# One DRAIN on GpSimd in front of the last expert's output DMAs, in an attention and mixture-of-experts kernel

## The chip, the core and the metric

The kernel runs on one core of one Trainium2 chip. The metric is the device time of one execution in microseconds (us). Each core has five engines with an instruction queue each: TensorE (PE: matrix products, with PEld for its weight loads), VectorE (DVE), ScalarE (ACT), GpSimd (POOL) and SyncE (SP, which here only issues DMAs). Engines wait for each other and for DMAs through semaphores. In a profile a name with a "q" behind it (POOLq, SPq) means an instruction that the engine's sequencer handles by itself, such as a DRAIN or a wait for semaphores; these are not counted as busy time.

## What is computed

An attention without softmax, normalised by its root mean square, and behind it a layer of eight experts. Each token goes to one expert, by sorted scores, and no expert takes more than N/E = 576 tokens:

```python
kv = np.einsum('bhsd,bhse->bhde', k, v)            # batch 8, heads 8, seq 576, head_dim 64
out = np.einsum('bhsd,bhde->bhse', q, kv)
x = out / np.sqrt(np.mean(out * out, axis=-1, keepdims=True) + 1e-06) * g_norm
...
logits = x @ w_gate                                # N, D, E, F = 4608, 512, 8, 1024
order = np.argsort(-logits.flatten())              # greedy: best score first, 576 per expert
...
for e in range(E):
    mask = assigned == e
    h = np.maximum(x[mask] @ w1[e], 0.0)
    out[mask] = h @ w2[e]
```

All data are float32.

## The kernel before

The attention runs first and leaves its result in DRAM as `x_dram`. Then the experts run one after the other, `t` = 0 to 7, while the search for the next expert's tokens runs beside them. `layers(t)` is one expert: 576 tokens in five blocks of rows (four of 128 and one of 64), a first product with `w1` (in `one_layer`, line 1243), ReLU on ScalarE (line 1218), and a second product with `w2` (`second`, line 1203). Both products are done in quarters after Winograd's form of Strassen's scheme: seven products of halves take the place of eight, for which sums and differences of the quarters have to be made first.

Those sums are GpSimd's work: of `w1` (`weight_sums`, tile `sw`, line 1088), of `w2` (`sum_w2`, tile `tw`, line 1166) and of the hidden layer (`sums`, tile `sh`, line 1195). GpSimd also issues all indirect DMAs: five gathers of token rows for each expert (line 990, `xg<-x_dram`) and five scatters of finished rows for each expert (`put`, line 1171, `out_dram<-y_sb` or `y_rest`). That is 40 + 40 = 80 DMAs in the program. SyncE issues the plain DMAs, mostly of weights.

For TensorE, VectorE, ScalarE and SyncE the order of work is the order in which the program is written. For GpSimd it is written by hand: `in_order` links each of its instructions behind the one before, without a semaphore. Nothing else decides its order.

The change lies in `layers`, between the first and the second half of an expert. Behind `one_layer` the last two sums of `tw` are issued (`sum_w2(t, len(tw_of[t][1]))`), and then the second products run, in the order `m` = 1, 2, 6, 5, 64, 7, 4, 3 for the last expert. Product 64 is the block of 64 rows (line 1311); its result `y_rest` goes out by the first `put`. Products 4 and 3 finish the other four blocks, with a `put` each. For the last expert there are no gathers of a next one, so that behind the last two `tw` sums GpSimd's queue holds only these five `put`s and the end of the program.

The end of the program is not written in the kernel. The tool chain puts it there (line 1428 in the profile): each engine executes a DRAIN, SyncE first waits for the semaphores of all DMAs, and then all engines meet in a barrier; GpSimd clears the semaphores, and they meet once more.

Of the kernel before, what the change touches and what calls it, by code (L numbers as in the profile page):

```python
# [26 lines left out]
def kernel(  # L27
# [11 lines left out]
    nc = tc.nc  # L39
# [4 lines left out]
    E, _, F = moe_w1.shape  # L44
# [841 lines left out]
    def in_order(made):  # L886

        if on_pool:
            tc.add_manual_dep(made.ins, on_pool[-1],
                              mybir.DependencyInfo(mybir.DependencyClass.NoSync, mybir.DependencyReason.SCHED_ONLY),  # L890
                              reason="order on GpSimd")
        on_pool[:] = [made.ins.name]
# [285 lines left out]
    def layers(t):  # L1178
# [113 lines left out]
        for i in range(FH):  # L1292
            summed.pop((t, i))
        weights.pop(t)

        y_of = [moe.tile([P, 2, DM], FT, name="y_sb", tag="y", bufs=2) for _ in range(2)]

# [57 lines left out]
    with tc.manual_schedule(engines={PE, DVE, ACTE, SPE}):  # L1355
# [31 lines left out]
        for t in range(E):  # L1387
            after = None
            for used in layers(t):
                if used == 0:  # L1390
                    next(turning)
                    continue
                if used is None:

                    if t + 1 < E:
                        while listed <= t:
                            search()
                        after = after or (turn if t + 1 < RELAID else turn_relaid)(t + 1)
                        wait += next(after) or 0.0
                    continue  # L1400
                wait -= used
                while wait <= 0 and search():
                    pass
            done, turning = t, after
# [28 lines left out]
```

## Time and profile before

| | us |
|---|---|
| median of 3 runs | 632.99 |
| lowest, highest | 629.66, 642.17 |
| the profiled execution | 632.92 |
| its span, from the first to the last instruction | 631.1 |
| PE busy in the span | 591.7 (94%) |
| DVE, ACT, POOL busy | 395.0, 200.3, 386.6 |
| indirect DMAs on POOL | 80, of 0.91 to 1.35 us for the outgoing ones |
| mean granted TensorE clock | 0.966 of full speed |

The span is what the trace shows; the 1.8 us between it and the execution's own time lie around it. Busy time counts work of the engines alone. A tail in which only sequencers have instructions shows no busy engine, so it has to be read from the rows of the line that ends the program, with start and duration of each DRAIN. A DMA has two times: that of the instruction that issues it on GpSimd, and its landing, which is given apart, from the issue on.

### The profile page before, as it was taken

To read this page: it belongs to the slowest core of one execution; us is meant where nothing else is said; L and a number is where in the kernel's file an instruction comes from. 1 tells how busy PE (TensorE), PEld (TensorE's weight loads), DVE (VectorE), ACT (ScalarE), POOL (GpSimd) and SP (SyncE) were. 2 spreads that over 40 slices of the span, in tenths; PEclk is the share of its full clock that TensorE was granted. 3 is DMA by queue.
4 is the path that set the end of the run, shared out by engine and by line. 5 is a ranking of instruction groups with operands and counts; after the bars stand their busy time and mean duration, and the time that the engine had idled before them with its cause. 6 is when DMAs were issued, how large, how long until landed. Compare 5 with 4: busy or idle time off the path is not lost.

```text
span 631.1 us, 12717 instructions
## 1 busy us (share of the span) xinstructions
PE 591.7 (94%) x4844; PEld 459.0 (73%) x4844; DVE 395.0 (63%) x1262; ACT 200.3 (32%) x428; POOL 386.6 (61%) x402
## 2 busy tenths in 40 slices
PE   8998999349999999999999999999999999999993
PEld 4777887226787678777867787778678877877873
DVE  4466669776786778579648867876993452242211
ACT  1565667913321222223222322231223213222310
POOL 0136444005875598479747886876778688788532
PEclk9999999559999999999999999999999999999998
DMA  8999999438018208224521574458145662731001
GB/s 274 296 323 308 318 315 357 175 119 269 6 37 310 71 2 270 79 69 133 164 81 44 171 205 148 136 190 209 42 168 183 176 204 69 219 110 43 2 8 66
DMA packets 60733, 100.46 MB, mean 159 GB/s; under 512 B 4608, under 2 KB 30208, under 8 KB 60160
## 3 DMA queue, kind: packets, MB, share of 16 engines
q1 hardware_dynamic: 54080, 80.75, 39.3%
q0 software_dynamic: 5888, 18.88, 9.3%
q8 instruction: 38, 0.62, 0.4%
q14 instruction: 23, 0.19, 0.1%
q10 hardware_dynamic: 704, 0.02, 0.1%
HBM read 76.04 MB, written 23.59 MB: 158 GB/s over the span
## 4 chain that ended last, share of the span: by engine, by line
PE 82%; DVE 8%; issue 4%; DMA 2%; POOL 2%; ACT 1%; POOLq 0%; SPq 0%; DVEq 0%; ACTq 0%
PE x_ps L1243 14%; PE x_ps L1203 12%; PE z_ps L1243 10%; PE y_ps L1243 9%; PE y_ps L1203 8%; PE z_ps L1203 7%; PE o_ps L494 4%; PE y_ps L1311 4%; PE qt_ps L382 3%; PE kv_ps L397 3%; DMA v_sb<-in_v_dram 2%; PE t_ps L1102 1%; PE given_ps L679 1%; PE warm_ps L916 1%; PE given_ps L674 1%
## 5 line engine op out<-in xcount | busy, mean ns | idle before, releaser
L1248 ACT COPY h<-x_ps 128x288 f32<-128x288 f32 x93 | 37.1, 399 | 169.0 <-PE x_ps L1243 163.6
L1243 PE MATMUL x_ps<-xs,sw 128*128 128x288 f32 x248 | 71.2, 409 | 0.4 <-DVE xs L1115 0.4
L1088 POOL TENSOR_TENSOR sw<-w_sb 128x256 f32<-128x256 f32 x64 | 46.8, 731 | 35.5 <-DMA w_sb<-in_moe_w_dram 21.1
L1203 PE MATMUL x_ps<-tw,sh 128*128 128x256 f32 x256 | 60.7, 383 | 0.0
L1243 PEld LDWEIGHTS x_ps<-xs,sw 128*128 128x128 f32 x248 | 46.3, 190 | 13.7 <-issue 1.1
L1171 POOL DMA_INDIRECT out_dram<-y_sb,outs x32 | 32.3, 1010 | 33.7 <-DVE y_sb L1347 25.2
L1203 PEld LDWEIGHTS x_ps<-tw,sh 128*128 128x128 f32 x256 | 47.4, 190 | 7.0 <-issue 0.8
L1195 POOL TENSOR_TENSOR sh<-hid 128x512 f32<-128x512 f32 x32 | 40.6, 1270 | 18.5 <-ACT hid L1218 18.5
L1218 ACT ACTIVATE hid<-hid 128x576 f32<-128x576 f32 x64 | 43.8, 686 | 23.3 <-DVE hid L1257 13.8
L530 POOL TENSOR_TENSOR xo<-o_sb,inv 128x512 f32<-128x512 f32 x27 | 28.4, 1079 | 33.1 <-DVE inv L517 33.1
L990 POOL DMA_INDIRECT xg<-x_dram,ids x40 | 38.1, 952 | 15.5 <-issue 9.9
L1166 POOL TENSOR_TENSOR tw<-w_sb 128x512 f32<-128x512 f32 x32 | 40.0, 1274 | 6.7 <-DMA w_sb<-in_moe_w_dram 6.6
L1341 ACT COPY u<-x_ps 128x512 f32<-128x512 f32 x24 | 14.0, 585 | 91.8 <-PE x_ps L1203 71.1
L494 PE MATMUL o_ps<-kvx,qt 64*128 64x72 f32 (+1 forms) x640 | 39.2, 271 | 1.9 <-issue 1.9
L494 PEld LDWEIGHTS o_ps<-kvx,qt 64*128 64x128 f32 (+1 forms) x640 | 34.5, 178 | 7.4 <-issue 6.5
L1243 PE MATMUL z_ps<-xt,sw 128*128 128x288 f32 x128 | 38.3, 415 | 0.1
L1243 PE MATMUL x_ps<-xt,w_sb 128*128 128x288 f32 x124 | 37.6, 416 | 0.5 <-ACT xt L1107 0.5
L1243 PE MATMUL y_ps<-xt,w_sb 128*128 128x288 f32 x128 | 37.0, 409 | 0.0
L1243 PE MATMUL z_ps<-xs,sw 128*128 128x288 f32 x128 | 36.8, 409 | 0.0
L1243 PE MATMUL y_ps<-xs,w_sb 128*128 128x288 f32 x128 | 36.5, 407 | 0.0
L507 DVE TENSOR_REDUCE ms<-sq 128x8 f32<-128x512 f32 x36 | 24.3, 682 | 18.6 <-ACT sq L500 18.2
L1203 PE MATMUL z_ps<-w_sb,sh 128*128 128x256 f32 x128 | 31.9, 390 | 0.5 <-DVE y_sb L1337 0.5
(315 smaller groups left out, 1313.2 us busy)
## 6 DMA issues: line engine op xcount, KB each, us to landing
w_sb<-in_moe_w_dram SPq DMA_DIRECT2D x32, 512.0 KB, 6.8
w_sb<-in_moe_w_dram SPq DMA_DIRECT2D x8, 2048.0 KB, 8.5
k_sb<-in_k_dram SPq DMA_DIRECT2D x16, 576.0 KB, 5.8
v_sb<-in_v_dram SPq DMA_DIRECT2D x16, 576.0 KB, 5.7
q_sb<-in_q_dram SPq DMA_DIRECT2D x16, 576.0 KB, 5.6
x_dram<-xo SPq DMA_DIRECT2D x16, 512.0 KB, 3.9
bounce<-xg SPq DMA_DIRECT2D x4, 1024.0 KB, 4.0
xr<-bounce SPq DMA_DIRECT2D x16, 256.0 KB, 4.7
```

Source lines behind the costliest of these rows:

```text
L494: nc.tensor.matmul(o_ps[rows_at, rp, (2 * r2 + l) * W:(2 * r2 + l + 1) * W], lhsT=turned_q[bn][ks, l, block // 2:block // 2 + m].rearrange ...
L530: nc.gpsimd.tensor_tensor(xo[:, t], o_sb[:, t, :, 0:D], inv[:, t * H:(t + 1) * H].rearrange("p (h o) -> p h o", o=1).to_broadcast([P, H, D ...
L990: tokens = nc.gpsimd.indirect_dma_start(out=xg[0:nr, n], out_offset=None, in_=x_dram, in_offset=bass.IndirectOffsetOnAxis(ap=ids[0:nr, n:n ...
L1088: in_order(nc.gpsimd.tensor_tensor(o, x, y, op=op))
L1166: in_order(nc.gpsimd.tensor_tensor(o, x, y, op=AL.subtract))
L1171: put = nc.gpsimd.indirect_dma_start(out=out, out_offset=bass.IndirectOffsetOnAxis(ap=ids_of[t][0:nr, n:n + 1], axis=0), in_=y_sb[0:nr, :] ...
L1195: in_order(nc.gpsimd.tensor_tensor(o[:, ms], x[:, ms], y[:, ms], op=op))
L1203: nc.tensor.matmul(p_ps[:, n], lhsT=left[:, f, n * P:(n + 1) * P], rhs=right[:, f], start=first, stop=(f == FH - 1), skip_group_check=True)
L1218: nc.scalar.activation(both, both, ACT.Relu)
L1243: nc.tensor.matmul(p_ps, lhsT=lhs[:, r], rhs=rhs[:, r], start=(m in (1, 2, 4, 5) and r == 0), stop=(r == 1), skip_group_check=(m in (6, 7, ...
L1248: nc.scalar.copy(u, p_ps)
L1311: nc.tensor.matmul(y_ps[l * nr:(l + 1) * nr], lhsT=hid[:, l * FH + f, a:a + nr], rhs=w2[:, l * FH + f, :], start=(f == 0), stop=(f == FH - 1))
```

## The change

For the last expert alone (`t + 1 == E`), one `drain` is issued on GpSimd. It is put in GpSimd's written order with `in_order`, behind the last two `tw` sums and in front of the five output DMAs. It has no semaphore to wait for, and no other instruction waits for it. The instructions of all engines, their order and their waits are otherwise the same as before.

```diff
@@ -1292,6 +1292,8 @@
         for i in range(FH):
             summed.pop((t, i))
         weights.pop(t)
+        if t + 1 == E:
+            in_order(nc.gpsimd.drain())
 
         y_of = [moe.tile([P, 2, DM], FT, name="y_sb", tag="y", bufs=2) for _ in range(2)]
```

## The prediction

> **What bounds the kernel now.** I read the page's chain by engine first, to see what sets the 631.1 us as a whole, and then only the last 40 us, because that is where the change sits.
>
> ```profile
> PE 82%; DVE 8%; issue 4%; DMA 2%; POOL 2%; ACT 1%; POOLq 0%; SPq 0%; DVEq 0%; ACTq 0%
> ```
>
> TensorE carries the span. The change adds and moves nothing on TensorE, so it can be worth something only in the few us in which TensorE is not working. Next, busy time by stretches, from the last hidden sums to the end (columns: length, then busy us of PE, PEld, DVE, ACT, POOL with counts, clock, DMA share, GB/s):
>
> ```profile
> 592.00:604.00 12.00, 12.00 (x57) 10.45 (x56) 1.92 (x4) 2.69 (x5) 7.43 (x6) 1.00 0.01 2
> 604.00:612.00 8.00, 8.00 (x37) 4.68 (x36) 0.67 (x1) 0.84 (x2) 0.00 (x0) 1.00 0.00 0
> 612.00:624.00 12.00, 9.49 (x43) 7.71 (x41) 2.24 (x5) 0.59 (x1) 4.76 (x5) 1.00 0.22 76
> 624.00:631.10 7.10, 0.00 (x0) 0.00 (x0) 0.00 (x0) 0.00 (x0) 0.00 (x0) 0.58 0.10 37
> ```
>
> Two things are to be seen. In the last 7.1 us no engine computes at all. And between 604 and 612 GpSimd does nothing, while TensorE is busy for every one of the 8 us. The timeline of GpSimd gives the order there (start, us, what, idle before):
>
> ```profile
> 601.31 2.49 POOL L1166 TENSOR_TENSOR tw<-tw,w_sb 128x512 f32<-128x512 f32 x2
> 612.29 0.91 POOL L1171 DMA_INDIRECT out_dram<-y_rest,outs  x1 [8.50 <-DVE y_rest L1319]
> 618.77 0.98 POOL L1171 DMA_INDIRECT out_dram<-y_sb,outs  x1 [5.57 <-DVE y_sb L1347]
> 620.06 0.96 POOL L1171 DMA_INDIRECT out_dram<-y_sb,outs  x1 [0.31 <-issue]
> 621.33 0.96 POOL L1171 DMA_INDIRECT out_dram<-y_sb,outs  x1 [0.30 <-issue]
> 622.75 0.95 POOL L1171 DMA_INDIRECT out_dram<-y_sb,outs  x1 [0.47 <-DVE y_sb L1337]
> ```
>
> The last sum ends at 601.31 + 2.49 = 603.80. The first output DMA cannot go before 612.01, when `y_rest` is written (VectorE, 611.33 + 0.68). The last output DMA is issued by 623.70. The tile view of the output in this window gives its landing:
>
> ```profile
> DMA to landing us min/median/max: 2.6/2.7/2.7
> ```
>
> So the data is in memory at 622.75 + 2.7 = 625.45, and yet the span runs to 631.1. What fills it are instructions of the sequencers, which do not count as busy. The view of line 1428 (end of the program; duration min/median/max in ns, first and last start):
>
> ```profile
> L1428 SPq EVENT_SEMAPHORE  x12: 17/28/28, 624.0 to 631.1; - x12
> L1428 POOLq EVENT_SEMAPHORE  x4: 17/17/17, 630.4 to 631.0; - x4
> L1428 POOLq DRAIN  x3: 40/107/7797, 622.5 to 630.9; - x3
> ```
>
> **GpSimd's closing DRAIN lasts 7797 ns**, from 622.5 to 630.3. The same view cut to 624 to 630 shows what else happens:
>
> ```profile
> L1428 SPq EVENT_SEMAPHORE  x10: 17/28/28, 624.0 to 626.0; - x10
> L1428 SPq DRAIN  x2: 7/7/7, 626.0 to 626.1; - x2
> ```
>
> SyncE has checked every DMA by 626.1 and then stands still until 630.4. The list of waits gives SyncE a wait of 4.4 us "for PEq", but TensorE was long done; GpSimd's DRAIN is what came last. So 630.3 − 626.1 = 4.2 us of the end belong to this DRAIN alone.
>
> **What the Trainium skill says.** "PSUM — Partial Sum Buffer", Engine vs sequencer instructions: a drain waits for the engine to go fully idle. The trace agrees that it waits, and shows more: the DRAIN goes on for 630.3 − 623.7 = 6.6 us after GpSimd's last recorded work. "Perfetto Trace Analysis", Sequencer-only Instruction: the time reported for a DRAIN is its execution, waits on semaphores not included; so the 7797 ns are work or waiting inside the DRAIN. "VectorE: DVE Perf Modes", The DRAIN you can't avoid, gives the closing DRAINs on all engines as about 12 ns. The trace has 7 to 19 ns for the later ones on the other engines, but 40 and 107 ns on GpSimd behind the long one, and 7797 ns for that one; the measurement decides. "DMA: Bandwidth & Descriptors", Anatomy of one DMA: about 2.0 us plus the bytes at 436 GB/s, an estimate of 2.6 us for the 256 KB of one output DMA; the trace has 2.7.
>
> **The change, part by part.** One instruction is added on GpSimd, behind the last two `tw` sums and in front of the five output DMAs of the last expert. No instruction of another engine moves, nothing waits for the DRAIN on another engine, and the DRAIN waits for no semaphore. Behind it on its queue stand only the five output DMAs and the closing DRAIN.
>
> (a) What the long DRAIN pays for. The first DRAIN of the program, before any DMA was issued, lasted little:
>
> ```profile
> L1419 POOLq DRAIN  x1: 188/188/188, 0.3 to 0.3; - x1
> ```
>
> So a DRAIN has no large fixed price (188, 107, 40 ns). Landing explains it up to 625.45; 630.3 − 625.45 = 4.85 us are left, in which no engine and no output transfer has anything to do. I choose: it is bookkeeping that has piled up over the kernel and is done by the next DRAIN, whichever that is. The likely unit is the indirect DMA: 40 gathers, 32 + 8 output DMAs, 80 in all. Counted from the landing that is 4.85 / 80 = 0.061 us each; counted from GpSimd's last work, 6.6 / 80 = 0.083 us each. It is not paid behind each DMA: issues stand 1.27 us apart, and a sum follows an output DMA within 1 us (561.78, then 562.77).
>
> (b) What the early DRAIN costs. 75 of the 80 DMAs stand in front of it: 75 x 0.061 = 4.6 us, or 75 x 0.083 = 6.2 us. It can end only when the sums have, at 603.80, so it ends at 608.4 to 610.0. Bounds: from nothing (it finds nothing to do) to the full 7.8 us, which gives 611.6. All lie ahead of 612.01, so it costs 0. The cover is GpSimd's idle time under TensorE's `x_ps`, `z_ps` and `y_ps` products. If that cover were overrun, the first output DMA would slip, and it has another 618.54 − 613.21 = 5.3 us before it is in the second's way.
>
> (c) What the closing DRAIN becomes. Five DMAs: 5 x 0.061 = 0.3 us behind the landing, so 625.45 + 0.3 = 625.8. That is ahead of SyncE's 626.1, which now is last. The part behind it (two barriers and the clearing of semaphores), 631.1 − 630.3 = 0.8 us, stays. Span: 626.1 + 0.8 = 626.9.
>
> Sum: 631.1 − 626.9 = **4.2 us** less. A gain above this is excluded, since SyncE's checks don't depend on the DRAIN. Against the profiled execution's own time, 632.92 (1.8 us around the span): 632.92 − 4.2 = 628.7. That execution is 0.07 us below the median of the three runs, 632.99, so the forecast against the median is the same, **628.7**. It is 0.7%; about 2% is what a measurement of this kernel can tell from no change.
>
> **Rivals.** (1) *The tail belongs to the last DMAs.* The 4.85 us are a fixed price of closing behind an output DMA just issued, or the early DRAIN returns at once and clears nothing. For it: the one long DRAIN is also the only one behind fresh DMAs, so the trace of before doesn't separate the two. Against it: the landing is over, and nothing of the kind shows between DMAs. Time: unchanged, 632.9.
>
> (2) *Part of it.* Some of the 4.85 us is piled up and some is not. Half each leaves the closing DRAIN ending at 625.45 + 2.4 = 627.9 instead of 630.3: 630.5.
>
> (3) *Slower: the early DRAIN overruns its cover.* It holds GpSimd's queue, and the output DMAs behind it then bunch at 1.27 us each. The last one is late when the first goes later than 622.75 − 4 x 1.27 = 617.7, so when the DRAIN lasts over some 13.6 us from 603.80. At twice the long DRAIN, 15.6 us, it ends at 619.4; the first DMA starts 0.3 later and the last at 624.8, 2.0 us late. With the closing DRAIN as long as before: 634.9. Against it: 13.6 us is nearly twice the longest DRAIN seen, with fewer DMAs in front.
>
> **How the numbers follow.** Piled-up work, all moved: 0.72, 628.7. Part: 0.08, 630.5. Nothing: 0.14, 632.9. Slower: 0.06, 634.9. The three runs of before reach from 629.66 to 642.17, more than the effect itself. So the low end is the lowest run less the gain, 629.66 − 4.2, rounded to 625.4. The high end takes in the case of no change with 1.6 us of spread, 634.5; a lone run like the 642.17 is left out. No case reaches 2% (620.3 or 645.6) by itself; only spread could: faster 0.01, same 0.97, slower 0.02.
>
> **What would show it.** A second long DRAIN on GpSimd at the changed line, some 4.5 us or more from 603.80 and done before 612; the first output DMA still at 612.3 and the last at 622.8; the closing DRAIN about 3 us instead of 7.8; SyncE's last check at 626.1, with its barrier directly behind. I am wrong if the closing DRAIN still takes 7 to 8 us (rival 1), if the output DMAs start later (rival 3), or if the closing DRAIN shrinks and the span doesn't, which would mean that something the trace doesn't show ends there too.

## The result, and the profile after

| | before | with the DRAIN |
|---|---|---|
| median of 21 runs, us | 634.24 | 630.97 |
| lowest, highest | 629.51, 648.46 | 626.15, 636.14 |
| ratio, 95% interval | | 0.9945 (0.9921 to 0.9970) |
| span of the profiled execution | 631.1 | 629.4 |
| tail: end of VectorE's last instruction to end of span | 8.65 | 4.42 |

The ratio is worth 3.5 us of 634.24 (1.9 to 5.0 by the interval). The ratio leaves out the slow executions, those more than 1.5% above the fastest of their kernel, so it is not quite the quotient of the two medians. Both ends of the interval are gains, though single runs scatter by more than that. The last row of the table is a sharper measure, and it is used for all runs below: VectorE's last instruction ends at 622.47 before and at 625.01 with the change, and what follows is only the last output DMA and the closing of the program. The two instructions, first before, then with the change (start, us):

```profile
622.05 0.42 DVE L1337 TENSOR_TENSOR y_sb<-z_ps,u 128x256 f32<-128x256 f32 x1 [2.09 <-PE z_ps L1203]
624.58 0.42 DVE L1339 TENSOR_TENSOR y_sb<-z_ps,u 128x256 f32<-128x256 f32 x1 [2.09 <-PE z_ps L1203]
```

The added DRAIN is the only row of its line in the changed kernel (engine, count, duration min/median/max in ns, first and last start):

```profile
L1296 POOLq DRAIN  x1: 11082/11082/11082, 601.5 to 601.5; - x1
```

It has to be read beside GpSimd's timeline (start, us, what, idle before):

```profile
603.85 2.50 POOL L1166 TENSOR_TENSOR tw<-tw,w_sb 128x512 f32<-128x512 f32 x2
614.83 0.92 POOL L1171 DMA_INDIRECT out_dram<-y_rest,outs  x1 [8.48 <-DVE y_rest L1321]
625.28 0.96 POOL L1171 DMA_INDIRECT out_dram<-y_sb,outs  x1 [0.47 <-DVE y_sb L1339]
```

The sequencer reaches the DRAIN at 601.48, while the sums in front of it are still running. The last of them ends at 606.35. So of the 11.08 us the first 4.87 are a wait for the engine, and the DRAIN's own part is 612.56 − 606.35 = **6.22 us**. The first output DMA is due at 614.6, and it still shows VectorE's `y_rest` as what it waited for: the DRAIN was done 2.0 us earlier.

The end of the program in the changed kernel:

```profile
L1430 SPq EVENT_SEMAPHORE  x12: 17/28/28, 626.6 to 629.4; - x12
L1430 POOLq EVENT_SEMAPHORE  x4: 17/17/17, 628.7 to 629.3; - x4
L1430 POOLq DRAIN  x3: 46/107/3196, 625.1 to 629.2; - x3
L1430 SPq DRAIN  x3: 7/7/7, 628.6 to 628.9; - x3
```

The closing DRAIN lasts 3196 ns instead of 7797. It ends at 628.25, and SyncE's own closing DRAIN comes at 628.6: now SyncE is last. The list of SyncE's waits has, for the wait that the prediction put down to GpSimd's DRAIN, 0.5 us at most, where it had 4.4:

```profile
SPq L1430 <- DMA out_dram<-y_sb,outs: 74.7, 2, 73.2
SPq L1430 <- PEq L1430: 0.7, 2, 0.5
```

The tail is 4.23 us shorter, and yet the span only 1.7. The other 2.5 us were lost long before the change could act. Over the first 100 us, in which the attention loads its data, the windows of the two profiles (length, then busy us and count of PE, PEld, DVE, ACT, POOL, clock, DMA share, GB/s) are, first before, then with the change:

```profile
0.00:100.00 100.00, 92.97 (x2004) 74.97 (x2005) 61.34 (x199) 54.86 (x107) 37.44 (x49) 0.98 0.91 309
```

```profile
0.00:100.00 100.00, 89.91 (x1969) 74.40 (x1978) 61.43 (x196) 52.80 (x103) 36.25 (x48) 0.97 0.91 303
```

TensorE has 35 matmuls fewer on record by then (10 of them are missing from the whole profile). Compared instruction by instruction, VectorE is 2.6 us late at 103 us and 2.5 us late at the end. The change cannot have caused this, since its DRAIN starts at 601.48. It is scatter of the loading stage, which moves from run to run: in the second profile of the same kernel (experiment 7) VectorE is 0.2 us late at that place.

### The profile page after: what moved, and what is told of

Its sections match the earlier page's. It is cut to its first block, busy times and chain, and to the rows that moved or that the text cites. A ratio compares the mean times of both kernels' runs of the same rounds, so it can differ in the third digit from the quotient of the medians.

```text
span 629.4 us, 12708 instructions
## 1 busy us (share of the span) xinstructions
PE 590.6 (94%) x4834; PEld 460.2 (73%) x4844; DVE 396.2 (63%) x1262; ACT 200.6 (32%) x428; POOL 387.4 (62%) x402
## 4 chain that ended last, share of the span: by engine, by line
PE 83%; DVE 6%; DMA 4%; issue 4%; POOL 2%; ACT 1%; POOLq 0%; SPq 0%; ACTq 0%; DVEq 0%
PE x_ps L1243 15%; PE x_ps L1203 12%; PE z_ps L1243 10%; PE y_ps L1243 10%; PE y_ps L1203 8%; PE z_ps L1203 7%; PE o_ps L494 5%; PE y_ps L1313 4%; DMA v_sb<-in_v_dram 3%; PE qt_ps L382 3%; PE kv_ps L397 3%; PE t_ps L1102 1%; PE given_ps L679 1%; PE given_ps L674 1%; PE warm_ps L916 1%
## 5 line engine op out<-in xcount | busy, mean ns | idle before, releaser
L494 PE MATMUL o_ps<-kvx,qt 64*128 64x72 f32 (+1 forms) x640 | 40.5, 276 | 0.9 <-PE kv_ps L397 0.4
L494 PEld LDWEIGHTS o_ps<-kvx,qt 64*128 64x128 f32 (+1 forms) x640 | 35.9, 183 | 6.0 <-issue 4.7
```

Of the source, the lines that this page charges most:

```text
L494: nc.tensor.matmul(o_ps[rows_at, rp, (2 * r2 + l) * W:(2 * r2 + l + 1) * W], lhsT=turned_q[bn][ks, l, block // 2:block // 2 + m].rearrange ...
```

## The experiments

The theory: a DRAIN on GpSimd works off something that piles up with each indirect DMA, some 0.083 us for each, and it can be done under TensorE's products. Against it stand a fixed price of a late DRAIN, work that piles up with every GpSimd instruction or with bytes, and a tail that belongs to the last output DMAs. "From idle" below is the time from the end of GpSimd's last instruction in front of the DRAIN to the DRAIN's end, from the trace's times.

**1. A DRAIN in every expert.** The condition is dropped:

```diff
-        if t + 1 == E:
-            in_order(nc.gpsimd.drain())
+        in_order(nc.gpsimd.drain())
```

> The DRAIN stands at the same place in all eight experts. Tail means here: from the end of VectorE's last instruction to the end of the span (8.65 us before, 4.43 with the change). Piled-up work per indirect DMA (0.083 us each, counted from the moment GpSimd's last earlier instruction ends): 10 DMAs lie between two DRAINs, so 0.8 us each for the first seven (more where the last gather has not landed yet), 0.4 us for the eighth with 5 DMAs in front, the closing DRAIN as in the changed kernel, tail 4.4 us, and a time like that of the changed kernel (ratio to before 0.992 to 1.000). Piled-up work per GpSimd instruction of any kind (0.0165 us each for 402): about 1.6 us for the first DRAIN (some 100 instructions in front), 0.7 us for the eighth (43 in front). A fixed price of a DRAIN that comes late after another (6 us each, however much is in front): 6 us for each of the eight, and the time goes up by 10 us or more, since the sums behind the first seven are needed soon.

Measured: ratio 0.9945 (0.9917 to 0.9973), tail 4.42 us. The DMAs in front of each of the eight turned out to be 5, 10, 15, 10, 10, 10, 10 and 5. From idle: 0.50, 0.90, 3.18, 0.89, 0.89, 0.89, 0.89 and 0.48 us. The third stands right behind a gather, whose issue ends at 318.37 and which lands at 320.89; it ends at 321.54, behind that landing. In front of the others every DMA has landed before GpSimd is idle. The row of the fifth, and the sums in front of it:

```profile
L1295 POOLq DRAIN  x1: 5752/5752/5752, 432.6 to 432.6; - x1
```

```profile
434.95 2.50 POOL L1166 TENSOR_TENSOR tw<-tw,w_sb 128x512 f32<-128x512 f32 x2
```

The reader sees how little a DRAIN's duration alone says: 5.75 us, of which all but 438.33 − 437.45 = 0.89 us is waiting for sums. The fixed price falls: it would have been 6 us eight times. So does the price by GpSimd instruction: the first DRAIN has 89 instructions and 5 DMAs in front of it and takes 0.50 us (0.0165 x 89 would be 1.5), the eighth 39 and 5 and takes 0.48 (0.64 by instructions).

**2. The DRAIN in the fourth expert only.**

```diff
-        if t + 1 == E:
+        if t == 3:
```

> One DRAIN as in the change, but in the fourth expert instead of the last. Piled-up work per indirect DMA: 40 DMAs in front of it, so it lasts 40 x 0.083 = 3.3 us from GpSimd's last earlier instruction, and the closing DRAIN has the other 40 to do: it ends 3.3 us after the last output DMA was issued (6.6 before, 2.0 with the change), tail 8.65 - 3.3 = 5.3 us. If the first long DRAIN of a program pays a fixed price that later ones don't, wherever it stands: it lasts some 6 us, and the tail is that of the changed kernel, 4.4 us. If the tail belonged to the last output DMAs: tail 8.65 us.

Measured: ratio 0.9966 (0.9937 to 0.9994), tail 5.48 us. The DRAIN takes 3.36 us from idle for its 40 DMAs, and the closing one 3.43 us for the other 40. The rows of the two:

```profile
L1296 POOLq DRAIN  x1: 8228/8228/8228, 374.4 to 374.4; - x1
```

```profile
L1430 POOLq DRAIN  x3: 46/107/4618, 627.3 to 632.5; - x3
```

An early DRAIN therefore doesn't make later ones cheap as such. It does its share, and what comes after it is left to the closing one. The reading that the tail belongs to the last output DMAs falls here, since these were the same five.

**3. The DRAIN where nothing covers it**, in front of the last output DMA, and not at the place of the change:

```diff
                 if m == 3 and t + 1 == E and f == FH - 1:
                     nc.vector.tensor_tensor(quarter(0, 1)[:, n], p_ps[:, n], u_of[6][:, n], op=AL.add)
+                    if n == 1:
+                        in_order(nc.gpsimd.drain())
                     put(t, n, P, y_of[0][:, n])
```

> The DRAIN stands between the fourth and the fifth of the last five output DMAs, where nothing covers it. Piled-up work per indirect DMA: 79 x 0.083 = 6.5 us from the end of the fourth output DMA; the fifth is issued some 6.3 us later than before, lands 2.7 us behind its start, and the closing DRAIN is short: tail 10.7 us instead of 8.65, that is 2 us slower than before and 6 us slower than the change (ratio to before about 1.003). If the early DRAIN clears nothing: tail 8.7 us or a little more, as before.

Measured: ratio 1.0012 (0.9978 to 1.0046), tail 11.27 us. The time does not tell it from before; the tail does, by 2.6 us. GpSimd's timeline there:

```profile
625.48 0.96 POOL L1171 DMA_INDIRECT out_dram<-y_sb,outs  x1 [0.31 <-issue]
633.76 0.96 POOL L1171 DMA_INDIRECT out_dram<-y_sb,outs  x1 [7.32 <-issue]
```

Of the 7.32 us between the two, the DRAIN with 79 DMAs takes 6.53, as the theory had it. The rest is new: the DMA behind it begins 0.79 us after the DRAIN's end, where 0.25 had been put in, and that is why the tail is 0.5 us longer than expected. The closing DRAIN has one DMA left, which lands at 636.47. It ends at 636.56, 1.84 us from idle:

```profile
L1430 POOLq DRAIN  x3: 46/107/3012, 633.5 to 637.6; - x3
```

**4. More DMAs with hardly more rows**, and no DRAIN added. The 16 extra gathers fetch rows that nothing uses:

```diff
                 rows_of[t, n] = xg[:, n]
+                if n < 2:
+                    in_order(nc.gpsimd.indirect_dma_start(
+                        out=more[:, n], out_offset=None, in_=x_dram,
+                        in_offset=bass.IndirectOffsetOnAxis(ap=ids[0:16, n:n + 1], axis=0)))
```

> The kernel before with no DRAIN added, but with 16 more gathers of 16 rows each (two for each expert, into a tile that nothing reads): 96 indirect DMAs instead of 80, rows up by 3% only. Piled-up work per indirect DMA: the closing DRAIN ends 96 x 0.083 = 7.9 us after the last output DMA was issued (6.6 before), tail 10.0 us. Piled-up work per row or per byte: 6.8 us and 8.85. A fixed price: 6.6 us and 8.65, as before.

Measured in one run: 661.85 us, tail 9.97 us. The closing DRAIN and the last output DMA:

```profile
L1433 POOLq DRAIN  x3: 46/107/9103, 650.1 to 659.8; - x3
```

```profile
650.36 0.96 POOL L1176 DMA_INDIRECT out_dram<-y_sb,outs  x1 [0.46 <-DVE y_sb L1342]
```

From idle, at 651.32, it takes 7.91 us, to two digits what 96 DMAs were to cost. A gather of 16 rows counts as much as one of 128, so neither rows nor bytes set the price. The whole run was 24 us above the median of the runs of before beside it, 637.6, and 1.3 us of that are in the tail. Against the profile of before, VectorE's last instruction is 27.6 us late. Of this, 9.2 us are there before the first gather is issued, in the first 100 us, where this run shows a granted clock of 0.88 and before shows 0.98. The other 18 us come while the experts run, and their cause is open. Only the tail of this run is used here.

**5. The DRAIN one output DMA later**, behind the first of the last five, and not at the place of the change:

```diff
                 put(t, NB - 1, nr, y_sb)
+                if t + 1 == E:
+                    in_order(nc.gpsimd.drain())
                 continue
```

> The DRAIN stands one output DMA later than in the change: behind the first of the last five, where only the 5.3 us until the second cover it. The runs so far give a DRAIN's length from GpSimd's last earlier instruction as 0.07 + 0.0817 us for each indirect DMA since the DRAIN before. With 76 DMAs: 6.3 us, so it overruns its cover by 1.0 us; in the run with the DRAIN in front of the last output DMA the next DMA also began 0.8 us behind the DRAIN's end, instead of 0.25. So the second output DMA begins 7.1 us behind the end of the first (5.6 before), 1.5 us late; the others follow at 1.27 us each and the last begins 1.35 us later, measured from VectorE's last instruction. Tail 4.42 + 1.35 = 5.8 us; ratio to before about 0.9955. If an overrun were taken up by the 5.3 us of slack between the output DMAs (the prediction's reading): tail 4.4 us. If the DRAIN must also wait until the first output DMA has landed before it counts: 2.7 + 6.3 = 9.0 us behind the start of that DMA, tail 7.6 us.

Measured: ratio 0.9970 (0.9943 to 0.9997), tail 5.78 us. The timeline:

```profile
611.03 0.92 POOL L1171 DMA_INDIRECT out_dram<-y_rest,outs  x1 [8.47 <-DVE y_rest L1319]
619.02 0.98 POOL L1171 DMA_INDIRECT out_dram<-y_sb,outs  x1 [7.08 <-DVE y_sb L1339]
620.30 0.96 POOL L1171 DMA_INDIRECT out_dram<-y_sb,outs  x1 [0.30 <-issue]
621.57 0.96 POOL L1171 DMA_INDIRECT out_dram<-y_sb,outs  x1 [0.30 <-DVE y_sb L1339]
622.84 0.96 POOL L1171 DMA_INDIRECT out_dram<-y_sb,outs  x1 [0.30 <-issue]
```

The DRAIN ends at 618.23, 6.28 us from idle. Behind it the output DMAs run back to back at 1.27 us each, and the last is issued late. The closing DRAIN has four DMAs left. The last lands at 625.56 and the DRAIN ends at 625.77:

```profile
L1430 POOLq DRAIN  x3: 46/107/4509, 621.3 to 626.7; - x3
```

The 7.08 us of idle are put down to line 1339 on VectorE, but this DMA sends what line 1349 wrote, and that had ended at 617.24: the wait was for the DRAIN, which is not a row of this view. One DMA's place costs 5.78 − 4.42 = 1.36 us.

**6 and 8. What is last with the change.** Thirteen waits are put on SyncE's queue early, for DMAs that have long landed, so that they need not be checked at the end; the DRAIN stays (`settled` collects the last DMAs of SyncE and the output DMAs of the expert before):

```diff
                 put(t, NB - 1, nr, y_sb)
+                if t + 1 == E:
+                    for made in settled[-13:]:
+                        seen = nc.sync.nop(nofuse=True)
+                        tc.add_manual_dep(seen.ins, made.ins.name,
+                                          mybir.DependencyInfo(mybir.DependencyClass.Sync, mybir.DependencyReason.DATA),
+                                          reason="SyncE sees what has landed")
                 continue
```

> The change, and beside it 13 waits on SyncE's queue, in the program behind the last weights, for DMAs that have landed long before the end. The closing list of checks then is four instead of nine behind the last output DMA. If SyncE's checks are what ends last in the changed kernel, the end now follows the closing DRAIN instead, 0.23 us behind the landing, and the tail is 4.42 - 0.37 = 4.05 us. If the closing DRAIN or the barrier were what ends last, the tail stays 4.42. In the time 0.4 us (0.06%) is too little to be told from the change.

> The kernel with SyncE's early checks once more, for a second profile. If SyncE's list of checks was what ended last with the change: four checks behind the last output DMA, the end follows the closing DRAIN, tail 4.05 us again. If the first tail was chance: a tail of 4.4 us.

Measured: tail 4.05 and 4.04 us. The end of the second of the two runs:

```profile
L1439 SPq EVENT_SEMAPHORE  x6: 17/28/28, 623.1 to 628.0; - x6
L1439 POOLq EVENT_SEMAPHORE  x4: 17/17/17, 627.3 to 628.0; - x4
L1439 POOLq DRAIN  x3: 46/107/3186, 624.1 to 627.8; - x3
L1439 SPq DRAIN  x3: 7/7/7, 627.1 to 627.5; - x3
```

SyncE has six such rows instead of twelve and is through at 627.1; GpSimd's DRAIN ends behind it, at 627.26, and the barrier follows at once. So SyncE's checks were what the change had left as last, and were worth 0.37 to 0.38 us (4.42 − 4.05 or 4.04). In the time (ratio 0.9931, 0.9900 to 0.9961) it can't be told from the change run beside it.

**7. The change again.**

> The change itself once more, beside the kernel that it is compared with. Piled-up work per indirect DMA: the early DRAIN ends 6.2 us behind the last sum, before the first output DMA is due; tail 4.4 us; ratio to before 0.992 to 0.997. If the first profile was chance: another length of the early DRAIN, or a tail other than 4.4.

Measured: ratio 0.9930 (0.9903 to 0.9956), tail 4.42 us; the early DRAIN takes 6.22 us from idle, the closing one ends 2.00 us from idle. Here the span is 627.8 us: the tail repeats to 0.01 us, while what lies in front of it does not. The early DRAIN's row:

```profile
L1296 POOLq DRAIN  x1: 11082/11082/11082, 599.9 to 599.9; - x1
```

Taken together, from idle and without the closing DRAINs of one, four and five DMAs and the third DRAIN of experiment 1, which end just behind a landing:

| indirect DMAs since the DRAIN before | 5 | 10 | 40 | 40 | 75 | 76 | 79 | 80 | 96 |
|---|---|---|---|---|---|---|---|---|---|
| us from idle | 0.48 | 0.89 | 3.36 | 3.43 | 6.22 | 6.28 | 6.53 | 6.61 | 7.91 |
| 0.07 + 0.0817 each | 0.48 | 0.89 | 3.34 | 3.34 | 6.20 | 6.28 | 6.52 | 6.61 | 7.91 |

The line was fitted to the runs up to experiment 4, and the 6.28 us of experiment 5 came after it. The 3.43 us, 0.09 above the line, are those of the closing DRAIN of experiment 2. It and the DRAINs left out of the table show something more when they are counted from the landing of the last DMA in front of them (DRAIN's end minus landing, from the trace's times):

| indirect DMAs since the DRAIN before | 1 (exp. 3) | 4 (exp. 5) | 5 (the change) | 15 (exp. 1, third) | 40 (exp. 2, closing) |
|---|---|---|---|---|---|
| us behind the landing | 0.08 | 0.21 | 0.25 | 0.65 | 1.68 |
| 0.042 + 0.0408 each | 0.08 | 0.21 | 0.25 | 0.65 | 1.67 |

So some 0.041 us for each DMA, half of the 0.0817, come behind the landing. That the other half is done before it, from idle on, fits: for 40 DMAs half of the work is over some 1.7 us from idle, and the landing in experiment 2 comes at 1.76. With 80 DMAs the landing, 1.74 us from idle, comes in the middle of the first half, and the DRAIN isn't held up by it. This reading in two halves is made from the figures afterwards; no run was made to test it.

## Why the prediction was right

- **The bound.** That only the tail could gain is borne out: in the profiles nothing in front of it answers to the change, and the tail went from 8.65 to 4.42 us.
- **(a) What the long DRAIN pays for.** Piled-up work by indirect DMA was right, and experiments 1, 2 and 4 show it against each other reading tried: a fixed price, the instructions, the rows, the last DMAs. Of the two prices given, 0.061 us counted from the landing and 0.083 counted from idle, the second is right: 0.0817. The prediction's 0.061 took it that no work is done before the landing. In the closing DRAIN of before, the work starts when GpSimd is idle and 1.74 of the 6.61 us lie beside that landing.
- **(b) The early DRAIN.** 6.2 us was the upper of the two estimates, and 6.22 were measured, done 2.0 us ahead of the first output DMA. At no cost, as stated. The cover was called from 603.80 to 612.01; its size, 8.2 us, held.
- **(c) The closing DRAIN.** 0.3 us behind the landing was expected, 0.25 measured (0.23 from the start of SyncE's check of that landing, the figure in the expectations). The form of the term, a price for each of the five DMAs behind the landing, is right: the second table above shows it. The price was not: 5 x 0.061 stands for 0.04 + 5 x 0.041. That two errors, the price and the missing 0.04, partly cancel is luck. It made no difference to the span, since SyncE is last, as said, and experiments 6 and 8 show that it is.
- **The sum.** 4.2 us were forecast for the tail, 4.23 measured, and 4.23 again in the second profile (8.65 − 4.42). Between whole runs the gain is 3.5 us with an interval that takes in 4.2. The forecast of 628.7 us was made against three runs of before with a median of 632.99; over 21 runs that median is 634.24, 1.25 us higher, which is over half of the 2.3 us between 628.7 and the 630.97 measured. The range that went with it, 625.4 to 634.5, holds even the 634.24 of before, so the time alone says little for the mechanism; the rows of the tail do. The 2% that the prediction took as the least that can be told from no change was too much: over these runs 0.55% can (the interval ends at 0.9970).
- **The rivals.** (1) and (2) fell with experiments 2 and 4. (3), overrun, doesn't happen at the place chosen, but its mechanism is real: in experiment 5, with less cover, the output DMAs bunch at 1.27 us each, and in experiment 3, with none, the last one is late. The step in its working that was mis-sized is the start of the DMA behind the DRAIN, put at 0.3 us, measured at 0.79.

What GpSimd does for each DMA in a DRAIN was not shown. The prediction's word for it, bookkeeping, is argued from the time it takes and from what it doesn't depend on.

## What to carry to other kernels

Where no engine works in the last microseconds, look at the sequencers' rows of the program's last line: one long DRAIN there can be the whole tail. On GpSimd count the indirect DMAs of the kernel; if they are many, one DRAIN in front of the last few, in a place where GpSimd waits anyway for longer than 0.08 us times their number, takes the price off the end. Leave room for the DMA behind it too, which starts 0.79 us after the DRAIN's end. What comes after the DRAIN stays at the end: with five DMAs left the closing DRAIN ended 0.25 us behind the landing, with 40 left 1.68 us. Then check the place: one DMA later it gave back a third of the gain, and in front of the last DMA more than all.

## What the runs showed of the hardware

- Where no landing held it up, a DRAIN on GpSimd took, from idle, 0.07 us and 0.0817 us for each indirect DMA since the DRAIN before, whether of 16 or 128 rows, and whether issued 60 us earlier or, in the kernel before, up to some 480 us; DRAINs with no new DMA took 40 to 189 ns.
- Its recorded duration includes the wait for GpSimd's instructions in front (4.87 of 11.08 us), and it also waits for DMAs in flight: five DMAs took 0.48 to 0.50 us from idle where all had landed, and 2.00 us in the closing DRAIN, whose last DMA landed 1.76 us from idle. Behind the last landing it took 0.08, 0.21, 0.25, 0.65 and 1.68 us for 1, 4, 5, 15 and 40 DMAs, that is 0.04 us and 0.041 us for each.
- An indirect DMA directly behind a DRAIN began 0.79 us after the DRAIN's end (experiments 3 and 5), where DMAs in a row follow each other's end by 0.30.
